# Attention probabilities transposed on VectorE in 32x32 blocks and regrouped by DMA, instead of on TensorE

## The chip, the cores and the metric

The kernel runs on one core of one Trainium2 chip. A core has five engines with instruction queues of their own: TensorE (PE, matrix products, with its weight loads shown as PEld), VectorE (DVE), ScalarE (ACT), GpSimd (POOL) and SyncE (SP), which here issues all DMAs. They work on one on-chip memory of 128 partitions (SBUF) and on a smaller accumulator memory (PSUM), in eight banks, that TensorE writes. The metric is the device time of one execution in microseconds (us); less is better.

## The reference

Eight batches of block-causal attention, eight heads of 64 columns over 576 positions in blocks of 64, followed by a gated feed-forward that also mixes positions. All data are float32.

```python
def _attn_ref(q, k, v):
    B, H, S, D = q.shape                      # 8, 8, 576, 64
    scores = 1.0 / np.sqrt(D) * np.matmul(q, k.transpose(0, 1, 3, 2))
    mask = block_i >= block_j                 # blocks of 64 positions
    scores = np.where(mask, scores, -1000000000.0)
    attn = np.exp(scores - np.max(scores, axis=-1, keepdims=True))
    attn = attn / (np.sum(attn, axis=-1, keepdims=True) + 1e-09)
    return np.matmul(attn, v)

def _moe_ref(x, w_in, w_spatial, b_spatial, w_out):
    h = np.maximum(x @ w_in, 0.0)             # 512 -> 1024
    u, v = h[..., :512], h[..., 512:]
    v_n = (v - mean(v)) / np.sqrt(var(v) + 1e-06)
    v_s = np.einsum('ts,bsd->btd', w_spatial, v_n) + b_spatial[None, :, None]
    return (u * v_s) @ w_out
```

## The kernel before

The work is cut into 32 head pairs (eight batches of four). For a pair the 576 query rows stand in four tiles of 128 and one of 64, and `SLOTS` lists seven pieces of score rows: for each of the two heads the tiles 0 and 1 together (slots 0 and 1), tile 2 (slots 2, 3), tile 3 (slots 4, 5), and for both heads together the last 64 rows (slot 6). Tile t needs only the first t + 1 blocks of 128 keys.

For each slot, `scores` (L265, and `scores_last`, L277) multiplies queries by keys into a PSUM bank `s`. In batch 0 it does so in float32 from the raw input; from batch 1 on `prep_pair` splits queries and keys into a high and a low part (`hi`, `lo`), and three products in float32r replace one. `exps` has DVE take the row minimum of the negated scores while it copies them to an SBUF tile `p` (L296, L305) and ACT apply the exponential with a running sum (L312). `norm` adds a small constant and inverts the sum on DVE (L321, L324) and has POOL scale `p` (L326). `p` then holds query rows in the partitions, but the product with `v` sums over keys, which must stand in the partitions. So `transposes` has TensorE turn each 128x128 block of `p` by a product with the identity (L352, L366) into a PSUM bank `t`; DVE (slots 0 and 1) or ACT copies the bank to the SBUF tiles `ptlo` and `pthi` (L354, L356, L361, and L367 for the last 64 keys). `av` multiplies them by `v` into the banks `avl` (query rows 0 to 255) and `avh` (256 to 575) (L396, L405), and `x_evac` brings these to the tile `x`, again as a high and a low part (L382, L383).

Once a batch's four pairs are there, `moe` makes a list of 29 groups of matrix products for its feed-forward: five `v_group` (bank `mv`; L436 and L447, then a relu, mean, variance and a scaling on L477, a cast to `vh` on L484 and the remainder `vl` on L485), eight `u_group` (bank `mu`, L505), eight `sp_group` (bank `ms`, L528, L532, L533; the mixing of positions) and eight `out_group` (bank `mo`, L549), whose results go out through `outT` (L555, L556).

The main loop walks over steps n, seven to a pair. A step issues one slot's `exps`, the `norm` of the slot before, the `transposes` of the slot before that, at certain steps scores or `av` (step 2 of the next pair, `RUN2`), loads, and about one feed-forward group of the batch before, so that the feed-forward of batch b runs between the attention of batch b + 1. In batch 0 there is no such work, and the weights are loaded and split in the background. The building framework, which orders each engine's instructions when the program is built, keeps roughly to this order but moves instructions where by its own account an operand comes late. On the chip each engine then works its list off in order. Tiles come from pools with a fixed number of buffers: seven for `p`, one for `ptlo` and `pthi`, one for the raw queries and keys, two for `v`, four PSUM banks for `s`, two for `t`, `avl` and `avh`, two for the feed-forward. A DMA is told finished by one of eight semaphores in turn, so that the ninth waits for the first.

Of the kernel before, what the change touches and what calls it, by code (L numbers as in the profile page):

```python
# [10 lines left out]
F32 = mybir.dt.float32  # L11
F32R = mybir.dt.float32r
I32 = mybir.dt.int32
AF = mybir.ActivationFunctionType
# [18 lines left out]
RUN2, LAST = 2, 5  # L33
# [3 lines left out]
def kernel(  # L37
# [25 lines left out]
    p_p = ctx.enter_context(tc.tile_pool(name="p_p", bufs=7))  # L63
    pt_p = ctx.enter_context(tc.tile_pool(name="pt_p", bufs=1))
# [36 lines left out]
    c4 = const.tile([P, P], F32, name="c4")  # L101
    nc.gpsimd.memset(c4[64:P, :], 0.0)
# [181 lines left out]
    def exps(b, pr, i):  # L284
# [3 lines left out]
        ssum = st_p.tile([P, 4], F32, tag="ssum", name=f"ssum_{nm}")  # L288
# [22 lines left out]
        for r, (o, n, mx) in enumerate(runs):  # L311
            nc.scalar.activation(  # L312
                pt[:, o:o + n], pt[:, o:o + n], AF.Exp, bias=mx, scale=-1.0,
                accum_out=ssum[:, r:r + 1],
            )
        ptiles[(b, pr, i)] = (pt, ssum, runs)

    def norm(b, pr, i):
        pt, ssum, runs = ptiles[(b, pr, i)]
        n = len(runs)  # L320
        nc.vector.tensor_scalar(  # L321
            out=ssum[:, 0:n], in0=ssum[:, 0:n], scalar1=EPS_SM, scalar2=None, op0=ALU.add
        )
        nc.vector.reciprocal(ssum[:, 2:2 + n], ssum[:, 0:n])  # L324
        for r, (o, n, mx) in enumerate(runs):
            nc.gpsimd.tensor_scalar(  # L326
                out=pt[:, o:o + n], in0=pt[:, o:o + n], scalar1=ssum[:, 2 + r:3 + r],
                scalar2=1.0, op0=ALU.mult, op1=ALU.mult,
            )

    pts = {}

    def pt_tiles(b, pr):
        if (b, pr) not in pts:
            lo = pt_p.tile([P, 2, 384], F32, tag="ptlo", name=f"ptlo_{b}_{pr}")
            hi = pt_p.tile([P, 2, 4, 320], F32, tag="pthi", name=f"pthi_{b}_{pr}")
            pts[(b, pr)] = (lo, hi)
        return pts[(b, pr)]

    def transposes(b, pr, i):  # L340
        hd, t0, t = SLOTS[i]
        pt = ptiles.pop((b, pr, i))[0]
        lo, hi = pt_tiles(b, pr)
# [5 lines left out]
        n = 3 if t == 1 else min(t + 1, 4)  # L349

        for c in range(n):
            nc.tensor.transpose(bk[:, c * P:(c + 1) * P], pt[:, c * P:(c + 1) * P], ident)  # L352
        if t == 1:
            (nc.scalar.copy if b == 0 else nc.vector.tensor_copy)(lo[:, hd, :], bk[:, 0:384])  # L354
        elif hd < 2:
            nc.scalar.copy(  # L356
                hi[:, hd, 0:n, (t - 2) * P:(t - 1) * P],
                bk[:, :n * P].rearrange("p (c q) -> p c q", q=P),
            )
        else:  # L360
            nc.scalar.copy(  # L361
                hi[:, :, :, 256:320].rearrange("p h c q -> p c h q"),
                bk.rearrange("p (c h q) -> p c h q", c=4, h=2),
            )
            bk = bank(f"{i}c4")
            nc.tensor.transpose(bk[0:64, 0:P], pt[:, 4 * P:S], ident)  # L366
            nc.scalar.copy(c4[0:64, :], bk[0:64, 0:P])  # L367
# [19 lines left out]
    def av(b, pr):  # L387

        lo, hi = pts.pop((b, pr))
# [3 lines left out]
        for c in range(2):  # L393
            for j in range(2):
                js = slice(64 * j, 64 * j + 64)
                nc.tensor.matmul(  # L396
                    al[js, c * P:256], vt[:, c, js],
                    lo[:, j, 0:256] if c == 0 else lo[:, j, 256:384],
                    start=(c == 0), stop=(c == 1),
                )  # L400
        for c in range(5):
            for j in range(2):
                js = slice(64 * j, 64 * j + 64)
                q0 = (0, 0, 0, 128, 256)[c]
                nc.tensor.matmul(  # L405
                    ah[js, q0:320], vt[:, c, js], hi[:, j, c, q0:] if c < 4 else c4[:, js],
                    start=(c == 0), stop=(c == 4),
                )
# [10 lines left out]
    def moe(b):  # L419
# [5 lines left out]
        def v_group(c):  # L425
# [16 lines left out]
            else:  # L442
# [34 lines left out]
            nc.vector.tensor_scalar(  # L477
                out=vr[:m, :], in0=vr[:m, :], scalar1=st[:m, 12:13], scalar2=st[:m, 13:14],
                op0=ALU.mult, op1=ALU.add,
            )  # L480
            if c < FULL:
                vh = ff_p.tile([P, DH], F32R, tag=f"vh{c}", name=f"vh_{b}_{c}")
                vl = ff_p.tile([P, DH], F32R, tag=f"vl{c}", name=f"vl_{b}_{c}")
                nc.vector.tensor_copy(vh, vr)  # L484
# [122 lines left out]
    def at(n):  # L607

        g, i = divmod(n, NS)
        return (*pairs[g], i) if 0 <= g < len(pairs) else None  # L610

    for n in range(N + 2 * NS):
# [17 lines left out]
        if at(n - 1):  # L630
            norm(*at(n - 1))
        if i == RUN2:
            if here:
                scores(*here, (4, 5))
            if 0 < g <= len(pairs):
                av(*pairs[g - 1])
                if g % NPAIR == 0:
                    gs = moe(pairs[g - 1][0])
                    queue += gs
                    rate = len(gs) / (NPAIR * NS)  # L640
# [8 lines left out]
        if at(n):  # L649
            exps(*at(n))  # L650
    for q in queue:
        q()
# [45 lines left out]
```

## Time and profile before

| | us |
|---|---|
| median of three runs | 773.93 |
| the three runs | 764.83, 773.93, 773.99 |
| the profiled execution | 765.58 |
| its span, first to last instruction | 763.8 |
| POOL busy in a steady batch (278.42 to 369.06) | 37.14 |
| granted TensorE clock, mean of the span | 0.996 |
| data moved by DMA | 48.63 MB, 64 GB/s |

A profile lists every instruction with its engine, its source line and its tiles as out<-in, its start and its duration, and for an engine that stood idle what ended the wait. Busy times of an engine are those in which it computes; a matmul's end is modelled, and following matmuls overlap, so that the sum of their durations is more than the time they take. The chain of waits follows the work that ended last back to its start, each step to what released it; there the times do add up. SPq is SP's list of DMA issues, which is not counted as busy.

### The profile page before, as it was taken

How to read it: one execution, taken by the hardware profiler on the slowest of the kernel's cores; microseconds unless marked ns; L12 is line 12 of the kernel's file. 1: busy time of each engine (PE TensorE's matmuls, PEld its weight loads, DVE VectorE, ACT ScalarE, POOL GpSimd, SP SyncE). 2: the span in 40 equal slices, each digit the busy share in tenths (PEclk: the TensorE clock that was granted, in tenths of full speed). 3: DMA queues.
4: the chain of work that ended last, by engine and by line, in shares of the span. 5: the costliest groups of instructions: out<-in, count | busy, mean ns of one | idle time of the engine just before them, and what ended most of it. 6: DMA issues, size and time to landing. Idle time of an engine off the chain costs nothing.

```text
span 763.8 us, 15854 instructions
## 1 busy us (share of the span) xinstructions
PE 740.3 (97%) x5508; PEld 636.0 (83%) x5508; DVE 471.9 (62%) x1743; ACT 436.1 (57%) x1236; POOL 318.4 (42%) x480
## 2 busy tenths in 40 slices
PE   8998889999999999999999999999999999999998
PEld 5556678987998878898888888898789987889898
DVE  6985984548745577547764577455874557742641
ACT  6885665656665556654655656564666555653232
POOL 4786465423444334442344423542344433431011
PEclk9999999999999999999999999999999999999999
DMA  6453231221122111221012211122112211000001
GB/s 215 151 170 103 84 98 33 75 82 34 52 69 72 42 51 51 69 71 58 18 51 82 78 38 50 30 71 84 33 52 73 67 42 51 18 33 32 1 9 55
DMA packets 21411, 48.63 MB, mean 64 GB/s; under 512 B 2386, under 2 KB 11090, under 8 KB 21332
## 3 DMA queue, kind: packets, MB, share of 16 engines
q1 hardware_dynamic: 21332, 47.63, 19.7%
q8 instruction: 44, 0.72, 0.4%
q14 instruction: 35, 0.29, 0.1%
HBM read 38.18 MB, written 9.44 MB: 62 GB/s over the span
## 4 chain that ended last, share of the span: by engine, by line
PE 81%; DVE 8%; ACT 5%; POOL 2%; issue 2%; DMA 1%; SPq 0%; ACTq 0%; DVEq 0%; POOLq 0%
PE mo L549 14%; PE ms L528 13%; PE mu L505 10%; PE t L352 10%; PE mv L436 10%; PE s L265 7%; PE avh L405 6%; PE s L277 3%; PE avl L396 2%; ACT p L312 2%; PE mv L447 1%; DVE st L457 1%; POOL p L326 1%; PE ms L533 1%; PE ms L532 1%
## 5 line engine op out<-in xcount | busy, mean ns | idle before, releaser
L326 POOL TENSOR_SCALAR p<-p,ssum 128x128 f32<-128x128 f32 (+4 forms) x288 | 177.9, 630 | 209.9 <-DVE ssum L324 173.9
L312 ACT ACTIVATE p<-p,nmax 128x128 f32<-128x128 f32 (+4 forms) x288 | 166.9, 581 | 59.6 <-DVE nmax L296 47.3
L296 DVE CUSTOM_DVE_ANT_0 p<-s,mask 128x128 f32<-128x128 f32 (+3 forms) x256 | 115.4, 484 | 62.8 <-PE s L265 62.7
L352 PE MATMUL t<-ident,p 128*128 128x128 f32 x768 | 124.6, 278 | 10.5 <-POOL p L326 7.2
L505 PE MATMUL mu<-x,wi_hi 128*128 128x288 f32 x512 | 116.5, 304 | 0.6 <-DVE vr L453 0.5
L352 PEld LDWEIGHTS t<-ident,p 128*128 128x128 f32 x768 | 90.6, 141 | 27.8 <-POOL p L326 12.3
L223 POOL TENSOR_TENSOR lo<-raw,hi 128x288 fp32r<-128x288 f32 (+1 forms) x84 | 66.9, 815 | 80.8 <-ACT hi L220 80.7
L436 PE MATMUL mv<-wi_hi,x 128*128 128x512 f32 x256 | 87.0, 401 | 0.0
L505 PEld LDWEIGHTS mu<-x,wi_hi 128*128 128x128 f32 x512 | 85.5, 188 | 1.4 <-DVE vr L453 0.7
L356 ACT COPY pthi<-t 128x512 f32<-128x512 f32 (+1 forms) x128 | 67.0, 525 | 29.1 <-PE t L352 28.8
L537 POOL TENSOR_TENSOR gl<-u,gh 128x288 fp32r<-128x288 f32 x48 | 38.7, 807 | 99.6 <-ACT gh L536 99.6
L528 PE MATMUL ms<-ws_hi,vh 128*128 128x288 f32 x256 | 80.0, 313 | 0.0
L535 DVE TENSOR_TENSOR u<-ms,u 128x288 f32<-128x288 f32 x64 | 29.3, 458 | 78.1 <-PE ms L533 78.0
L528 PE MATMUL ms<-ws_hi,vl 128*128 128x288 f32 x256 | 75.4, 294 | 0.0
L528 PE MATMUL ms<-ws_lo,vh 128*128 128x288 f32 x256 | 75.3, 294 | 0.0
L549 PE MATMUL mo<-gh,wo_hi 128*128 128x288 f32 x256 | 74.7, 315 | 0.0
L549 PE MATMUL mo<-gh,wo_lo 128*128 128x288 f32 x256 | 70.0, 295 | 0.0
L505 PE MATMUL mu<-x,wi_lo 128*128 128x288 f32 x256 | 69.7, 295 | 0.0
L536 ACT CAST gh<-u 128x288 fp32r<-128x288 f32 x64 | 27.8, 434 | 71.8 <-DVE u L535 71.8
L321 DVE TENSOR_SCALAR ssum<-ssum 128x1 f32<-128x1 f32 (+1 forms) x224 | 37.2, 166 | 50.8 <-ACT p L312 50.8
L405 PE MATMUL avh<-pthi,v 128*64 128x320 f32 (+1 forms) x512 | 67.9, 407 | 0.0
L405 PEld LDWEIGHTS avh<-pthi,v 128*64 128x64 f32 x512 | 36.0, 138 | 24.2 <-issue 0.3
(114 smaller groups left out, 1648.4 us busy)
## 6 DMA issues: line engine op xcount, KB each, us to landing
raw<-qk SPq DMA_DIRECT2D x31, 608.0 KB, 3.9
v<-v SPq DMA_DIRECT2D x32, 320.0 KB, 3.0
outT<-o SPq DMA_DIRECT2D x64, 144.0 KB, 1.8
rwi<-w_in SPq DMA_DIRECT2D x8, 512.0 KB, 4.6
rwo<-w_out SPq DMA_DIRECT2D x4, 512.0 KB, 3.7
rws<-w_spT SPq DMA_DIRECT2D x4, 288.0 KB, 2.7
rwt<-w_spT SPq DMA_DIRECT2D x2, 144.0 KB, 2.8
raw<-qk SPq DMA_DIRECT2D x2, 128.0 KB, 2.3
```

Source lines behind the costliest of these rows:

```text
L223: (nc.vector if n == 0 else nc.gpsimd).tensor_tensor(out=lo[:, cs], in0=raw[:, cs], in1=hi[:, cs].bitcast(F32), op=ALU.subtract)
L265: nc.tensor.matmul(banks[(b, pr, i + hd)][:, o:o + n], a[js, qs], k[js, :n], start=(m == 0), stop=(m == len(parts) - 1),)
L296: nc.vector.tensor_tensor_reduce(out=pt[:, o:o + n], in0=bk[:, o:o + n], in1=mask[:, 512 - n:], scale=-0.125, scalar=BIG, op0=ALU.add, op1 ...
L312: nc.scalar.activation(pt[:, o:o + n], pt[:, o:o + n], AF.Exp, bias=mx, scale=-1.0, accum_out=ssum[:, r:r + 1],)
L326: nc.gpsimd.tensor_scalar(out=pt[:, o:o + n], in0=pt[:, o:o + n], scalar1=ssum[:, 2 + r:3 + r], scalar2=1.0, op0=ALU.mult, op1=ALU.mult,)
L352: nc.tensor.transpose(bk[:, c * P:(c + 1) * P], pt[:, c * P:(c + 1) * P], ident)
L356: nc.scalar.copy(hi[:, hd, 0:n, (t - 2) * P:(t - 1) * P], bk[:, :n * P].rearrange("p (c q) -> p c q", q=P),)
L405: nc.tensor.matmul(ah[js, q0:320], vt[:, c, js], hi[:, j, c, q0:] if c < 4 else c4[:, js], start=(c == 0), stop=(c == 4),)
L436: nc.tensor.matmul(ps, xs[k][:, j, cs], w[:, k, DH:], start=(n == 0), stop=(n == 3 * NC - 1),)
L505: nc.tensor.matmul(ps[:, :HT], w[:, k, ds], xs[k][:, j, zs], start=(n == 0), stop=(n == 3 * NC - 1),)
L528: nc.tensor.matmul(ps[:, :HT], a[:, ds], w[:, k, zs], start=(n == 0), stop=False)
L549: nc.tensor.matmul(ps[:, :HT], w[:, k, es], a[:, k, :], start=(n == 0), stop=(n == 3 * ND - 1),)
```

## The change

From the second batch on TensorE transposes nothing. For those batches `transposes` has DVE transpose `p` in blocks of 32x32: each block is turned in place of its own 32 partitions, so what stands in partitions 32a to 32a + 31 comes from query rows 32a to 32a + 31, and the keys 32r to 32r + 31 of a block of 128 lie in column group r of the tiles `tlo` and `thi`. `exchange` then moves, for each of the four r and each of the four a, partitions 32a of column group r to partitions 32r, column group a of the tiles `dlo` and `dhi`: 16 DMAs each for the low part (slots 0 to 3) and the high part (slots 4 to 6), 32 a pair, from SBUF to SBUF, all issued by SP. In batch 0 `transposes_pe` still uses TensorE, and ACT writes its result in the new layout into the same `dlo` and `dhi`.

The other edits: `norm` and `transposes` take two slots at a time (the sums of the two heads share a tile), after the steps 1, 3, 5 and 6 of a pair. `av` reads `dlo` and `dhi` in runs of 32 columns, tile by tile, with 28 matmuls for 14, over the same number of columns, and is issued at step 4 of the next pair instead of 2 (`AV_AT`), in batch 0 still at 2. The ring of `p` has five buffers for seven; `tlo`, `thi`, `dlo` and `dhi` have one each. In `v_group` the scaling and the cast to `vh` go from DVE to ACT.

```diff
-RUN2, LAST = 2, 5
+RUN2, LAST, AV_AT = 2, 5, 4
+LB, HB = 6, 4
+LW, Q8O, HW = 2 * 32 * LB, 2 * 32 * HB, 2 * 32 * HB + 5 * 32
...
-    p_p = ctx.enter_context(tc.tile_pool(name="p_p", bufs=7))
-    pt_p = ctx.enter_context(tc.tile_pool(name="pt_p", bufs=1))
+    p_p = ctx.enter_context(tc.tile_pool(name="p_p", bufs=5))
+    tr_p = ctx.enter_context(tc.tile_pool(name="tr_p", bufs=1))
...
+    dlo = const.tile([P, 4, LW], F32, name="dlo")
+    dhi = const.tile([P, 4, HW], F32, name="dhi")
...
     def norm(b, pr, i):
+        both = [ptiles[(b, pr, j)] for j in ((i - 1, i) if i < NS - 1 else (i,))]
+        ssum = both[0][1]
+        n = sum(len(runs) for _, _, runs in both)
         nc.vector.tensor_scalar(
             out=ssum[:, 0:n], in0=ssum[:, 0:n], scalar1=EPS_SM, scalar2=None, op0=ALU.add
         )
-        nc.vector.reciprocal(ssum[:, 2:2 + n], ssum[:, 0:n])
+        nc.vector.reciprocal(ssum[:, 4:4 + n], ssum[:, 0:n])
...
+    def transposes(b, pr, i):
+        hd, t0, t1 = SLOTS[i]
+        pt = ptiles.pop((b, pr, i))[0]
+        if i == 0:
+            halves["lo"] = tr_p.tile([P, 4, LW], F32, tag="lo", name=f"tlo_{b}_{pr}")
+        if i == 4:
+            halves["hi"] = tr_p.tile([P, 4, HW], F32, tag="hi", name=f"thi_{b}_{pr}")
+        to, o, n = place(hd, t0)
+        to = halves["lo" if to is dlo else "hi"]
+        if t1 > t0:
+            n += t1 + 1
+        nc.vector.transpose(
+            to[:, :, o:o + 32 * n].rearrange("p r (c j) -> p c r j", j=32),
+            pt[:, :n * P].rearrange("p (c r j) -> p c r j", r=4, j=32),
+        )
+        if hd == 2:
+            nc.vector.transpose(
+                to[:, 0:2, Q8O + P:], pt[:, 4 * P:S].rearrange("p (r j) -> p r j", j=32)
+            )
+
+    def exchange(part):
+        t, d = halves[part], dlo if part == "lo" else dhi
+        for r in range(4):
+            w = LW if part == "lo" else HW if r < 2 else HW - 32
+            for a in range(4):
+                nc.sync.dma_start(d[32 * r:32 * r + 32, a, :w], t[32 * a:32 * a + 32, r, :w])
...
     def av(b, pr):
...
+        def tiles(t0, t1, c):
+            n = t1 - t0 + 1
+            out, q0 = (al, 0) if t1 < 2 else (ah, 2)
+            for j in range(2):
+                js = slice(64 * j, 64 * j + 64)
+                d, o, _ = place(j, t0)
+                o += 32 * c
+                nc.tensor.matmul(
+                    out[js, (t0 - q0) * P:(t1 + 1 - q0) * P].rearrange(
+                        "p (t a j) -> p a t j", a=4, j=32
+                    ),
+                    vt[:, c, js],
+                    d[:, :, o:o + 32 * n].rearrange("p a (t j) -> p a t j", j=32),
+                    start=(c == 0), stop=(c == t1),
+                )
...
-            nc.vector.tensor_scalar(
-                out=vr[:m, :], in0=vr[:m, :], scalar1=st[:m, 12:13], scalar2=st[:m, 13:14],
-                op0=ALU.mult, op1=ALU.add,
+            nc.scalar.activation(
+                vr[:m, :], vr[:m, :], AF.Identity, bias=st[:m, 13:14], scale=st[:m, 12:13]
             )
...
-                nc.vector.tensor_copy(vh, vr)
+                nc.scalar.copy(vh, vr)
...
-        if n >= 2 and at(n - 2):
-            transposes(*at(n - 2))
...
+        if at(n - 2) and at(n - 2)[0] > 0:
+            k = (i - 2) % NS
+            for j in (k - 1, k) if k in (1, 3, 5) else (k,) if k == 6 else ():
+                transposes(*at(n - 2)[:2], j)
+            if k in (3, 6):
+                exchange("lo" if k == 3 else "hi")
```

What this does to the order shows best on TensorE, VectorE and SyncE. Names carry the pair within the batch, then the slot or part (`t_2_0` is slot 0 of pair 2), and a running number.

TensorE before, in a steady batch: the whole `av` of pair 1 at one place, then the first transposes of pair 2 (`t`, from `p`) and a feed-forward group.

```order
L396 MATMUL avl_1_4036<-ptlo_1_3764,v_1_3299 64x256 x2
L396 MATMUL avl_1_4036<-ptlo_1_3764,v_1_3299 64x128 x2
L405 MATMUL avh_1_4037<-pthi_1_3765,v_1_3299 64x320 x6
L405 MATMUL avh_1_4037<-pthi_1_3765,v_1_3299 64x192 x2
L405 MATMUL avh_1_4037<-c_125,v_1_3299 64x64 x2
L352 MATMUL t_2_0_4060<-ident,p_2_0_3974 128x128 x3
L528 MATMUL ms_0_1_4065<-ws_hi,vh_0_3459 128x288
```

TensorE after, first place in the same batch: the part of pair 1's `av` that reads `dlo`, between two feed-forward groups.

```order
L588 MATMUL ms_0_2_4097<-ws_a,vs_a 128x288
L589 MATMUL ms_0_2_4097<-ws_b,vs_b 128x288
L444 MATMUL avl_1_4127<-dlo,v_1_3324 64x4x2x32 x2
L444 MATMUL avl_1_4127<-dlo,v_1_3324 64x128 x2
L444 MATMUL avh_1_4128<-dlo,v_1_3324 64x128 x6
L584 MATMUL ms_0_3_4163<-ws_hi,vh_0_3513 128x288
```

TensorE after, second place: the part that reads `dhi`, one `ms` group, the last scores of pair 2 and two `mo` groups later, among pair 3's first scores.

```order
L273 MATMUL s_3_2_4260<-hi_3_4009 128x384
L273 MATMUL s_3_3_4261<-hi_3_4009 128x384
L273 MATMUL s_3_2_4260<-lo_3_4010,hi_3_4009 128x384
L444 MATMUL avh_1_4128<-dhi,v_1_3324 64x128 x8
L461 MATMUL avh_1_4128<-dhi,v_1_3324 64x64 x10
L273 MATMUL s_3_3_4261<-lo_3_4010,hi_3_4009 128x384
```

The transposes are gone from TensorE's list, and `av` has become two pieces, each standing where its half of the exchange is expected. From the high part of one pair to that of the next there are, in this stretch, five `mo` groups, four `ms` groups, three runs of scores and one low part.

VectorE before, in the same batch: copies of slots 0 and 1 (`ptlo`) among the evacuations of `av` (`x`) and feed-forward work (`u`).

```order
L324 RECIPROCAL ssum_2_5_4186<-ssum_2_5_4186 128x1
L354 COPY ptlo_2_4058<-t_2_0_4060 128x384
L383 TENSOR_TENSOR x_1_4052<-avh_1_4037,x_1_4052 128x320
L535 TENSOR_TENSOR u_3426<-ms_0_1_4065,u_3426 128x288
L354 COPY ptlo_2_4058<-t_2_1_4093 128x384
```

VectorE after: the block transposes of pair 2's slots 4, 5 and 6 (`thi`), among the score reductions of pair 3 (`p`, `nmax`) and the evacuation of pair 1's `av`.

```order
L395 STREAM_TRANSPOSE thi_2_4310<-p_2_4_4183 128x4x4x32
L395 STREAM_TRANSPOSE thi_2_4310<-p_2_5_4211 128x4x4x32
L308 ISA p_3_1_4333,nmax_3_1_4332<-s_3_1_4259,mask 128x128
L308 ISA nmax_3_1_4332 128x1
L308 ISA p_3_1_4333,nmax_3_1_4332<-s_3_1_4259,mask 128x256
L308 ISA nmax_3_1_4332 128x1
L395 STREAM_TRANSPOSE thi_2_4310<-p_2_6_4254 128x4x4x32
L426 TENSOR_TENSOR x_1_4157<-avh_1_4128,x_1_4157 128x320
L400 STREAM_TRANSPOSE thi_2_4310<-p_2_6_4254 128x2x32
```

Copies from PSUM became transposes within SBUF, and the last of them stands behind the evacuation of an `av`.

SyncE before, in a steady batch: one load of queries and keys (`raw`) and one of `v` a pair, and the stores.

```order
L210 DMA raw_3_3947<-qk 128x1216
L232 DMA v_2_3641<-v 128x640
L210 DMA raw_0_4245<-qk 128x1216
L232 DMA v_3_3945<-v 128x640
L556 DMA outT<-o_0_0_4182 128x288
L210 DMA raw_1_4545<-qk 128x1216
```

SyncE after, in a steady batch, from one store to the next low exchange.

```order
L612 DMA outT<-o_0_0_2947 128x288
L410 DMA dlo<-tlo_2_2859 32x384 x6
L240 DMA v_3_2718<-v 128x640
L410 DMA dlo<-tlo_2_2859 32x384 x10
L612 DMA outT<-o_0_1_2989 128x288
L218 DMA raw_0_3022<-qk 128x1216
L612 DMA outT<-o_0_2_3040 128x288
L612 DMA outT<-o_0_3_3069 128x288
L410 DMA dhi<-thi_2_3050 32x416 x8
L410 DMA dhi<-thi_2_3050 32x384 x8
L410 DMA dlo<-tlo_3_3161 32x384 x6
```

Loads and stores now stand within and between the two exchanges of a pair, on the one list that SP works off in order; the load of `v` stands inside the low exchange and waits for a `v` buffer, which the high part of an `av` gives free.

More of the change, by code (lines that the diff above doesn't have):

```diff
@@ L287, in exps @@
         nmax = st_p.tile([P, 2], F32, tag="nmax", name=f"nmax_{nm}")
[L288 removed]
+        if hd == 1:
+            ssum = ptiles[(b, pr, i - 1)][1]
+        else:
+            ssum = st_p.tile([P, 8], F32, tag="ssum", name=f"ssum_{nm}")
+        s0 = hd * (t1 - t0 + 1) if hd < 2 else 0
         pt = p_p.tile([P, S], F32, tag="p", name=f"p_{nm}")
@@ L396, in av @@
                 nc.tensor.matmul(
[L397 to L406, printed above, removed]
+                    ah[js, 256:320].rearrange("p (a j) -> p a j", j=32), vt[:, c, js],
+                    dhi[:, 2 * j:2 * j + 2, Q8O + 32 * c:Q8O + 32 * c + 32],
                     start=(c == 0), stop=(c == 4),
```

95 lines of the change are left out of this document (49 added, 46 removed).

## The prediction

> **What bounds it now.** I read the page's busy times and its chain first, then the busy times by stretch, then the chain of waits in order of time inside one pair.
>
> ```profile
> span 763.8 us, 15854 instructions
> PE 740.3 (97%) x5508; PEld 636.0 (83%) x5508; DVE 471.9 (62%) x1743; ACT 436.1 (57%) x1236; POOL 318.4 (42%) x480
> PE 81%; DVE 8%; ACT 5%; POOL 2%; issue 2%; DMA 1%; SPq 0%; ACTq 0%; DVEq 0%; POOLq 0%
> ```
>
> TensorE (PE) is busy for 97% of the span and makes 81% of the chain that ended last. An average can hide stages, so the next view cuts the span where the first `av` of a batch starts. The columns are stretch, length, then busy time and count for PE, weight loads, DVE, ACT and POOL, then granted clock, DMA share and GB/s.
>
> ```profile
> 0.00:94.67 94.67, 82.39 (x463) 54.56 (x464) 74.47 (x278) 66.50 (x184) 61.06 (x83) 0.96 0.45 145
> 94.67:187.78 93.11, 89.77 (x697) 78.79 (x696) 59.63 (x218) 55.71 (x156) 45.50 (x68) 1.00 0.21 66
> 278.42:369.06 90.64, 89.82 (x695) 78.67 (x693) 56.24 (x214) 52.80 (x152) 37.14 (x59) 1.00 0.18 56
> 703.39:763.80 60.41, 56.76 (x389) 52.83 (x388) 23.43 (x59) 16.23 (x43) 5.13 (x7) 1.00 0.07 24
> ```
>
> The first stretch is mixed (PE idles 12 us). A steady batch lasts 90.64 us with PE idle for 0.8, DVE at 56.2 and DMA at 18%: there, an instruction taken from PE is time gained, as long as nothing else takes PE's place. The last stretch is feed-forward alone and has no transposes.
>
> The chain inside one pair of such a batch (start, length, engine and line) shows what a transpose costs next to its neighbours, which a busy time of overlapping matmuls can't.
>
> ```profile
> 302.22 0.48 PE t L352 x3
> 302.70 1.58 PE ms L528 x12
> 304.28 0.13 PE ms L532
> 304.41 0.14 PE ms L533
> 304.55 0.33 PE t L352 x3
> ...
> 308.89 0.79 PE s L277 x6
> 309.68 0.33 PE t L352 x3
> 310.01 1.58 PE mo L549 x12
> 311.59 0.44 PE t L352 x4
> ...
> 313.60 1.41 PE s L265 x17
> 315.00 0.59 PE t L352 x4
> ...
> 317.20 0.44 PE t L352 x4
> 317.63 0.11 PE t_6c L366
> ...
> 319.33 0.90 PE s L265 x4
> 320.23 0.80 PE avl L396 x8
> 321.03 2.05 PE avh L405 x20
> 323.09 0.26 PE t L352
> ```
>
> Three transposes take 0.33 us, four 0.44, the odd one 0.11. The 0.48 and 0.59 are the same groups behind an `av` and behind scores; I take the extra 0.15 as the price of leaving those, which whatever follows will pay.
>
> **The change, part by part.** *Transposes leave PE* in batches 1 to 7, 28 pairs. A pair has four groups of three (of the 0.33 rows there are three, the first and last shown, and the 0.48), three of four, and the odd one: 4 x 0.33 + 3 x 0.44 + 0.11 = 2.75 us, or 3.05 with the extras. 28 x 2.75 = 77 us off (85 at most). That the move happens isn't in doubt: from batch 1 on PE's order holds no transpose.
>
> *The value product `av`* streams the same 1600 columns per half-head pair, in 28 matmuls instead of 14. Rows: 1216 columns in 2.05 us, 1.69 ns each; the first 384 in 0.80, 2.08 ns each. At the first price nothing is added, at the second 0.6 us a pair. It now comes as two groups, so one more change of kind, 0.15. I take +0.25, 32 x 0.25 = +8, ends 0 and +20. No row shows a moving operand read in runs of 32 columns; at half speed it would cost 2.85 us a pair and eat the whole gain, but I have no row that suggests it.
>
> *DVE and ACT.* Rows give count, busy us and mean ns, by shape.
>
> ```profile
> L354 DVE COPY ptlo<-t 128x384 f32<-128x384 f32 x56 | 30.8, 551 | 22.7 <-PE t L352 22.7
> L477 DVE TENSOR_SCALAR vr<-vr,st 128x512 f32<-128x512 f32 x32 | 19.7, 617 | 0.6
> L484 DVE CAST vh<-vr 128x512 fp32r<-128x512 f32 x32 | 14.2, 443 | 0.6
> L321 DVE TENSOR_SCALAR ssum<-ssum 128x1 f32<-128x1 f32 x160 | 23.8, 149 | 41.5 <-ACT p L312 41.4
> L324 DVE RECIPROCAL ssum<-ssum 128x1 f32<-128x1 f32 x160 | 25.5, 160 | 4.0
> L296 DVE CUSTOM_DVE_ANT_0 p<-s,mask 128x512 f32<-128x512 f32 x64 | 42.2, 682 | 34.5 <-PE s L265 34.5
> L296 DVE CUSTOM_DVE_ANT_0 p<-s,mask 128x384 f32<-128x384 f32 x64 | 35.0, 549 | 0.1
> L150 DVE SCALAR_TENSOR_TENSOR fwo<-rwo,fwo 128x512 int32<-128x512 int32 x4 | 3.7, 922 | 0.0
> L356 ACT COPY pthi<-t 128x512 f32<-128x512 f32 x64 | 36.8, 575 | 3.1 <-PE t L352 3.0
> L441 ACT ACTIVATE vr<-mv 128x512 f32<-128x512 f32 x32 | 19.1, 597 | 51.4 <-PE mv L436 51.3
> ```
>
> Per batch DVE loses 8 copies (4.4 us), five scalings (about 3), four casts (1.8) and 12 of 28 add-and-reciprocal pairs of 0.31 (3.7): 12.9. It gains, per pair, four block transposes of 384 columns, three of 512 and one of 64. No row shows such a transpose. The ends are the 443 ns cast and the 922 ns three-operand form; I take the score reduction, the nearest single pass over as much data: 4 x 0.55 + 3 x 0.68 + 0.2 = 4.45 us, 17.8 per batch (12 to 27). So DVE goes from 56.2 to 61, of a batch of 90.64 - 4 x (2.75 - 0.25) = 80.6: room left, at the upper end 70, little. ACT loses 20 copies of up to 0.58 and gains nine passes of about 0.6: no more than before, 52.8 of 80.6, hidden behind PE.
>
> *The exchange* adds 32 DMAs per pair, all issued by SP, each 32 partitions of 1.5 KB. No DMA between SBUF addresses is in the trace. SP's issue times back to back (start, length, count), and landing times from issue:
>
> ```profile
> 0.72 1.81 SPq L208 DMA_DIRECT2D raw<-qk  x4
> 72.69 1.18 SPq L178 DMA_DIRECT2D rwt<-w_spT  x2
> 73.92 0.75 SPq L180 DMA_DIRECT2D rwt<-b_sp  x2
> outT<-o SPq DMA_DIRECT2D x64, 144.0 KB, 1.8
> rwt<-w_spT SPq DMA_DIRECT2D x2, 144.0 KB, 2.8
> ```
>
> One issue costs 0.45 (128 partitions), 0.59 (64) or 0.375 (one). I take 0.45, the row with most samples, and a landing of 2.0. With the raw load, the v load and two stores, 36 issues x 0.45 = 16.2 us of SP in a pair of 20.15 (80.6 / 4). It fits; at 0.59 it is 21.2 and doesn't.
>
> Busy time isn't enough, since SP serves in order. In a steady batch the `v` load of the pair after next stands inside the low exchange and waits for the high part of `av` (two v buffers). Behind it: 10 low DMAs, the raw load, three stores, then 16 high ones: 31 issues, 14.0 us, and 2.0 for landing: 16.0. In the same time PE has, from one high `av` to the next, five `mo` groups of 1.6, four `ms` of 1.85, scores of 0.90, 0.79 and 1.41, and 1.4 of low `av`: some 20 us. So the high exchange lands about 4 us early. The low one: 11 issues and landing, 6.95, against two `mo`, two `ms` and two scores, 8.6: 1.6 us early. Both hidden; without that cover each further microsecond stops PE.
>
> **A rule against the change.** The Trainium skill's page "VectorE: DVE Perf Modes" (section "Rules for kernel authors") advises TensorE for a 128x128 transpose whenever PSUM is an acceptable destination. By it the copies stay where they are and the sum is zero or a loss. For that to come true here DVE would have to become the bound: without transposes it has 43.3 us a batch, so they would have to take over 47 of 90.64, 2.6 times my rows; I count that within the chance of the DVE case below. The rows speak against it: PE has 0.8 us idle in a batch, DVE 34.
>
> **The sum**, against the profiled execution's own time of 765.58 us: -77 for the transposes, +8 for `av`. Batch 0 keeps its transposes and is not bound by PE: 0, ends -4 and +4 (12 small DVE pairs fewer; a ring of five probability tiles instead of seven). Batch 1 idles 3.3 us on weights, which won't shrink: +2. At the end the last high exchange (16 x 0.45 + 2.0 = 9.2) has only what feed-forward work can start without it: +2. In the steady batches closer engines and an in-order DVE that now waits for POOL before a transpose: +0.2 a pair, +6, ends 0 and 28. Sum 706.6, so 707 us. The median of the runs shown, 773.93, stands 1.1% above the profiled time; on that level the forecast is about 715.
>
> **Rivals.** *The exchange becomes the bound and the change is about even.* The loop runs from a high `av` through 31 issues and the landing to the next one, 31s + L + 1.4. It passes 20.15 at s = 0.54 with L = 2.0. At the 64-partition row (0.59, 2.8) it is 22.5 us, the old pair being 22.66: about 763. For it: the smaller transfer had the dearer issue. Against: one partition cost least.
>
> *The same loop, slower than before.* Above s = 0.595 (L = 2.8) a pair is longer than 22.66 whatever PE saves, and from 0.615 the loss passes 2%. If halving the partitions once more costs as much again as from 0.45 to 0.59, s = 0.73; at 0.65 the loop takes 24.4, 28 x 1.7 = 49 us more: 815. Nothing in the trace excludes it. The Trainium skill's page "DMA: Bandwidth & Descriptors" (section "Rules for kernel authors") says transfers under 64 KB are mostly overhead, and each DMA here moves 48 or 52 KB; the trace's four loads, issued 0.45 apart, show that such overheads overlap.
>
> *DVE.* If a block transpose costs like the 922 ns row, DVE has 70 of 80.6 us and its order makes PE wait for score banks; a microsecond a pair, 28 us: 735.
>
> **Chances.** Forecast 0.62, DVE 0.14, even 0.11, slower 0.13. The time is the forecast's, 707. The lower bound is the sum with every addition at its end of nothing, 688; upwards the range runs through the DVE case to the even one, 765, which leaves out the slower case, part of the even one and little below: 0.2. About 2% is what a measurement of this kernel can tell from no change, so faster takes the first two cases, 0.76; same 0.11; slower 0.13. For the forecast alone: 690 to 722.
>
> **What would show it.** Right: no L352-like rows after batch 0, a steady batch of 79 to 82 us, PE idle under 2 us in it, block transposes of 0.5 to 0.75 us, SP issues near 0.45. Wrong: PE idle in front of the high `av`, put down to a DMA; SP with gaps of 0.55 or more between issues; DVE above 65 us a batch; `av` above 3.2 us a pair.

## The result: slower by about 6%

The changed kernel takes 820.28 us (median of 4 runs, 814.8 to 823.25) against 770.23 for the kernel before on the same chips (4 runs, 764.83 to 773.99): a ratio of 1.0647, 95% interval [1.0547, 1.0748]. The forecast was 707 us, with a range up to 765. What came is nearest to the rival that the prediction called "the same loop, slower than before" and had put at 815 us for an issue of 0.65 us; how far that match goes is said under "The chances" below.

The head of the page of the changed kernel (busy time, share and instructions by engine) and its DMA issues (count, KB each, median us from issue to landing):

```profile
span 817.2 us, 17067 instructions
PE 722.1 (88%) x5704; PEld 612.6 (75%) x5704; DVE 501.2 (61%) x1647; ACT 424.2 (52%) x1140; POOL 307.3 (38%) x480
...
dlo<-tlo SPq DMA_DIRECT2D x448, 48.0 KB, 1.9
...
dhi<-thi SPq DMA_DIRECT2D x224, 52.0 KB, 2.3
dhi<-thi SPq DMA_DIRECT2D x224, 48.0 KB, 2.0
```

TensorE did lose its transposes, but its share fell from 97% to 88%: it now waits. The same columns as before, by stretch from one first `av` of a batch to the next, say where:

```profile
0.00:99.19 99.19, 87.32 (x575) 61.83 (x575) 76.09 (x246) 70.68 (x188) 58.35 (x82) 0.88 0.45 142
99.19:203.85 104.66, 92.42 (x705) 79.17 (x704) 66.61 (x215) 51.21 (x139) 42.63 (x66) 0.90 0.44 122
...
300.79:398.12 97.33, 86.16 (x705) 73.95 (x705) 61.03 (x206) 50.36 (x138) 35.77 (x58) 0.96 0.43 119
...
686.91:817.20 130.29, 113.12 (x907) 103.36 (x906) 54.83 (x167) 50.04 (x129) 27.14 (x43) 0.97 0.25 70
```

The first stretch is 4.5 us longer than before. Its 575 products, for 463, are mostly the smaller pieces of `av`, with two feed-forward groups more and 25 transposes fewer, so its edge lies a little later in the work. PE idles 11.9 us in it as against 12.3. A steady batch lasts 96.6 us on average (five from 203.85 to 686.91) against 90.64, with PE idle for 10 to 11 us instead of 0.8. DVE, at 61.0, has room.

What PE waits for, and what DVE waits for (engine, line, releaser: us in total, times, longest):

```profile
PE avl L444 <- DMA dlo<-tlo: 43.3, 8, 8.1
...
DVE tlo L395 <- DMA dlo<-tlo: 54.4, 19, 6.3
```

Both are the landing of the low exchange. That could be a slow transfer or a late issue; SP's list of issues between two low `av` of a steady batch (start, length from first to last, count) and PE's row behind it tell which:

```profile
441.20 10.30 SPq L410 DMA_DIRECT2D dhi<-thi  x16
451.61 3.70 SPq L410 DMA_DIRECT2D dlo<-tlo  x6
455.41 0.53 SPq L240 DMA_DIRECT2D v<-v  x1
455.98 6.20 SPq L410 DMA_DIRECT2D dlo<-tlo  x10
462.28 0.53 SPq L612 DMA_DIRECT2D outT<-o  x1
```

```profile
463.97 1.12 PE L444 MATMUL avl<-dlo,v 128*64 128x256 f32 x4 [5.10 <-DMA dlo<-tlo]
```

From 441.20 to 462.18 SP issues 33 DMAs without a pause, 20.98 us, 0.636 each. The last low one starts near 461.6 and lands 2 us later, and then `av` starts, 5.10 us after PE ran out of other work. The transfers are as quick as forecast (2.0 us); it is the issuing that is late.

That holds for all steady batches. From 203.85 to 686.91 the waits of SP's list add up to some 31 of 483 us; the longest of them, and the one for the high `av` in front of the `v` load, are:

```profile
SPq L612 <- ACT o L611: 11.7, 12, 1.8
...
SPq L240 <- PE avh L461: 0.7, 1, 0.7
```

So the queue itself is full: a pair of 24.15 us is 36 issues of 0.63 us, 22.7 us, and 1.5 us of waits.

### The profile page after: what moved, and what is told of

It is laid out like the page before. It is cut to its first block, busy times and chain, and to the rows that moved or that the text cites. A ratio compares the mean times of both kernels' runs of the same rounds, so it can differ in the third digit from the quotient of the medians.

```text
span 817.2 us, 17067 instructions
## 1 busy us (share of the span) xinstructions
PE 722.1 (88%) x5704; PEld 612.6 (75%) x5704; DVE 501.2 (61%) x1647; ACT 424.2 (52%) x1140; POOL 307.3 (38%) x480
## 5 line engine op out<-in xcount | busy, mean ns | idle before, releaser
L342 POOL TENSOR_SCALAR p<-p,ssum 128x128 f32<-128x128 f32 (+4 forms) x288 | 167.9, 598 | 119.0 <-DVE ssum L338 78.5
L561 PE MATMUL mu<-x,wi_hi 128*128 128x288 f32 x512 | 114.0, 303 | 11.1 <-ACT vr L498 6.6
L395 DVE STREAM_TRANSPOSE tlo<-p 128x384 f32<-128x384 f32 x112 | 60.9, 561 | 65.1 <-DMA dlo<-tlo 54.4
L444 PE MATMUL avl<-dlo,v 128*64 128x256 f32 (+1 forms) x256 | 32.6, 382 | 43.4 <-DMA dlo<-tlo 43.3
L470 POOL TENSOR_SCALAR xs<-x 128x128 fp32r<-128x128 f32 x32 | 10.3, 322 | 160.2 <-DVE x L426 160.2
L611 ACT COPY o<-mo 128x288 f32<-128x288 f32 x64 | 25.4, 397 | 83.7 <-DMA outT<-o 54.8
L493 PEld LDWEIGHTS mv<-wi_hi,x 128*128 128x128 f32 x256 | 49.2, 192 | 20.2 <-ACT x L425 5.4
L605 PEld LDWEIGHTS mo<-gh,wo_hi 128*128 128x128 f32 x256 | 48.9, 191 | 19.1 <-ACT gh L592 11.0
L395 DVE STREAM_TRANSPOSE thi<-p 128x512 f32<-128x512 f32 x84 | 54.1, 687 | 14.5 <-POOL p L342 4.8
L444 PEld LDWEIGHTS avl<-dlo,v 128*64 128x64 f32 x256 | 18.4, 154 | 56.4 <-issue 50.9
```

Of the source, the lines that this page charges most:

```text
L342: nc.gpsimd.tensor_scalar(out=pt[:, o:o + w], in0=pt[:, o:o + w], scalar1=ssum[:, r:r + 1], scalar2=1.0, op0=ALU.mult, op1=ALU.mult,)
L395: nc.vector.transpose(to[:, :, o:o + 32 * n].rearrange("p r (c j) -> p c r j", j=32), pt[:, :n * P].rearrange("p (c r j) -> p c r j", r=4, ...
L444: nc.tensor.matmul(out[js, (t0 - q0) * P:(t1 + 1 - q0) * P].rearrange("p (t a j) -> p a t j", a=4, j=32), vt[:, c, js], d[:, :, o:o + 32 * ...
L493: nc.tensor.matmul(ps, xs[k][:, j, cs], w[:, k, DH:], start=(n == 0), stop=(n == 3 * NC - 1),)
L561: nc.tensor.matmul(ps[:, :HT], w[:, k, ds], xs[k][:, j, zs], start=(n == 0), stop=(n == 3 * NC - 1),)
L605: nc.tensor.matmul(ps[:, :HT], w[:, k, es], a[:, k, :], start=(n == 0), stop=(n == 3 * ND - 1),)
```

## The experiments

Three theories stood against each other at first. A: SP's time to issue one DMA, about 0.63 us, is the bound, whatever the DMA carries. B: the data are the bound, that is the bytes, the landing or the short pieces. C: the other edits (block transposes on DVE, work moved to ACT, `av` in pieces) make the loss.

**Four wide copies for each exchange.** Column group r goes as it stands, all 128 partitions in one DMA: 8 DMAs a pair for 32, for nearly the same bytes (the last 32 columns of the high half are left out); the partitions aren't regrouped.

```diff
-            for a in range(4):
-                nc.sync.dma_start(d[32 * r:32 * r + 32, a, :w], t[32 * a:32 * a + 32, r, :w])
+            nc.sync.dma_start(d[:, r, :w], t[:, r, :w])
```

> Each exchange moves the same bytes with 4 DMAs over all 128 partitions instead of 16 over 32 (not regrouped, so the layout is not the one av wants; the last 32 columns of the high part are left out for all partitions). Theory A (SP's time to issue a DMA is the bound: 36 issues a pair, 0.63 us each for those of 32 partitions): 12 issues a pair at about 0.47, SP no longer matters, TensorE is the bound again, a steady batch of 79 to 82 us, 700 to 720 in all. Theory B (the data and their landing are the bound): the bytes stay, so the gain is half at most, above 760. Theory C (the other edits, DVE's order and TensorE's slower clock cost the time, not the exchange): no change, 800 to 825.

Measured: 739.97 us, beside 766.64 for the kernel before. One steady batch, and four of SP's issues in one row:

```profile
192.76:278.33 85.57, 81.37 (x705) 71.93 (x704) 61.33 (x205) 48.62 (x138) 35.06 (x58) 1.00 0.40 133
```

```profile
377.34 2.42 SPq L409 DMA_DIRECT2D dhi<-thi  x4
```

The batch falls from 96.6 to 85.57 us, and all the edits that C names are still in it, so C can't hold the bulk of the loss. The four issues still take some 0.6 us each (2.42 / 4), although each now has 128 partitions. But 740 isn't the 700 to 720 that A expected: A names the bound, and 20 us more are still to be explained (below).

One more thing differs, which the edit doesn't name. The building framework now places the high part of `av` straight behind the low one, which starts at 278.33 here; in the changed kernel it stands 14 us behind, after the low one at 439.68 (first row here, second there):

```profile
279.69 1.04 PE L443 MATMUL avh<-dhi,v 128*64 128x128 f32 x16
453.52 1.09 PE L444 MATMUL avh<-dhi,v 128*64 128x128 f32 x16
```

The gain could thus be partly one of order. The next run speaks against it: it has 32 DMAs again, the framework puts the two parts next to each other in about half of its pairs, and it is slow. In the runs after that the place varies too.

**The same count, wide.** 32 DMAs a pair again, each with 128 partitions and a quarter of the columns (no regrouping either).

```diff
-                nc.sync.dma_start(d[32 * r:32 * r + 32, a, :w], t[32 * a:32 * a + 32, r, :w])
+                nc.sync.dma_start(d[:, r, a * q:a * q + q], t[:, r, a * q:a * q + q])
```

> As many DMAs as in the change (32 a pair) and the same bytes, but each over 128 partitions and a quarter of the columns (not regrouped; the last 32 columns of the high part left out). Theory A with a price that hangs on the number of partitions: 0.47 per issue as for the 128-partition loads, 36 x 0.47 = 17 us a pair, 705 to 740. Theory A with a price for any DMA between SBUF addresses: 0.63 stays, 800 to 825. Theory B: quarter-size rows cost the DMA engines more, not less: 815 or above.

**A quarter of the bytes.** The DMAs of the change, with 96 columns each; the rest of `dlo` and `dhi` is not renewed.

```diff
-                nc.sync.dma_start(d[32 * r:32 * r + 32, a, :w], t[32 * a:32 * a + 32, r, :w])
+                nc.sync.dma_start(d[32 * r:32 * r + 32, a, :96], t[32 * a:32 * a + 32, r, :96])
```

> The 32 DMAs of 32 partitions a pair stay, but each moves 96 of 384 or 416 columns (three quarters of the regrouping is left out). Theory A: the number of issues and their 0.63 us stay, 805 to 825. Theory B: a quarter of the bytes, landings nearer 1.5 us than 2, SP waits less for its eight semaphores, below 760.

**Without the diagonal.** The 8 of the 32 DMAs that move partitions to themselves are left out.

```diff
+                if a != r:
-                nc.sync.dma_start(d[32 * r:32 * r + 32, a, :w], t[32 * a:32 * a + 32, r, :w])
+                    nc.sync.dma_start(d[32 * r:32 * r + 32, a, :w], t[32 * a:32 * a + 32, r, :w])
```

> The four DMAs of each exchange that keep their partitions (a equal to r) are left out: 24 a pair instead of 32. Theory A: 28 issues a pair x 0.63 = 17.7 us, plus waits of the order of those now, a pair of 20 to 21 instead of 24.3, 715 to 745. Theory B: a quarter of the bytes and landings goes too, but not the time of each: 780 to 800. Theory C: 805 to 825.

Measured: 842.05, 832.6 and 757.45 us, one run each. None is in A's bracket: the first is 17 us above it, at a time that B allows as well, the second 8 and the third 12 us above. What tells the theories apart is that a quarter of the bytes brings nothing where B expected less than 760, and the rows of issues. A row of 16 issues from each of the first two, and 12 from the third:

```profile
419.44 10.60 SPq L411 DMA_DIRECT2D dhi<-thi  x16
```

```profile
416.55 10.85 SPq L410 DMA_DIRECT2D dhi<-thi  x16
```

```profile
385.88 8.60 SPq L411 DMA_DIRECT2D dhi<-thi  x12
```

Sixteen issues take 10.3 us in the changed kernel, 10.60 with four times the partitions and a quarter of the columns, 10.85 with a quarter of the bytes (a few gaps included). A quarter of the bytes doesn't help at all, and a quarter fewer DMAs takes 63 us off the changed kernel's 820.28. B falls. The time goes by the number of DMAs, with the price of one the same from 12 to 192 KB and from 32 to 128 partitions. Why the first two are 12 to 22 us slower than the changed kernel isn't shown.

**Other queues.** In three runs other engines issued some of the 32. First ACT those with a = 3, 8 a pair:

```diff
-                nc.sync.dma_start(d[32 * r:32 * r + 32, a, :w], t[32 * a:32 * a + 32, r, :w])
+                (nc.scalar if a == 3 else nc.sync).dma_start(
+                    d[32 * r:32 * r + 32, a, :w], t[32 * a:32 * a + 32, r, :w]
+                )
```

> 8 of a pair's 32 regrouping DMAs are issued by ACT's queue. Theory A with a price of the issuing engine: SP 28 x 0.63 = 17.7 us of a pair, ACT gains 8 x 0.5 to 0.6 = 4 to 5 us a pair of instruction slots, in which its other work waits; 745 to 790 us, well below 820. Rival (the DMA engines or a shared ring are the limit, not the issuing queue): SP's interval grows as ACT's issues come in, 805 to 835 us.

785.78 us in one run: with the same DMAs and the same bytes 34 us below the changed kernel, so it is the issuing queue and not the engines that carry the data. The Trainium skill's page "DMA: Bandwidth & Descriptors" (section "Rules for kernel authors") says that spreading DMAs over issuing engines only saves sequencer issue time; here that saving was what counted, and it was worth those 34 us.

Then three queues, a = 2 by POOL and a = 3 by ACT:

```diff
+                (nc.sync, nc.sync, nc.gpsimd, nc.scalar)[a].dma_start(
```

> The 32 regrouping DMAs of a pair are issued by three queues: SP 16 (with its 4 loads and stores 20, at 0.63 us some 12 us of a pair), ACT 8 (at the 0.52 us seen with two queues, 4 us) and POOL 8. Theory A: no queue is the bound any more and the time comes to what the four wide copies gave, 740 to 760 us, below the 766 to 770 of the kernel before, if a POOL issue costs under 1 us. Rival Q (POOL's issues are dear, or its queue holds the normalisation of the probabilities up behind waits): 770 to 830 us, with TensorE waiting for POOL or for dhi.

770.99 us (10 runs) against 767.37: ratio 1.0036 [0.9993, 1.0079], no difference. That is 11 us above A's bracket, and at the lower edge of rival Q. Q's first reason fails, since POOL's issues were cheap (0.5 us each, by the first row below). Its second is not excluded: POOL stood 26.2 us in front of its own exchange issues (second row). PE's longest waits are not for POOL, though, but for ACT:

```profile
384.67 2.02 POOL L410 DMA_DIRECT2D dlo<-tlo  x4
```

```profile
POOL dhi L410 <- DVE thi L400: 26.2, 25, 1.3
```

```profile
PE mo L607 <- ACT gh L594: 12.9, 13, 2.1
PE ms L586 <- ACT o L613: 6.6, 8, 2.2
```

So the last of these left ACT alone: POOL issues a = 3 and half of a = 2, SP the other 20.

```diff
+                (nc.gpsimd if a == 3 or (a == 2 and r > 1) else nc.sync).dma_start(
```

> ACT issues none of the regrouping DMAs: SP 20 of a pair's 32 (24 with its loads and stores, 24 x 0.633 = 15.2 us of a pair, below the 20.15 us that the forecast wanted), POOL 12 (12 x 0.49 = 5.9 us beside its 9 us of work). Theory A2 (with three queues it was ACT's 8 issues, 8 x 0.54 = 4.3 us a pair, that made TensorE wait for ACT's gh and o): those waits fall from 12.9 and 6.6 us to under 4 each, a batch is 86 to 88 us and the run 740 to 760 us, faster than before by 1 to 4%. Rival: the waits move to the landing of dhi or to POOL's normalisation, 765 to 785 us, no gain.

777.92 us (6 runs) against 766.75: ratio 1.0136 [1.0092, 1.018]. The time is the rival's, no gain, though the waits it named (the landing of `dhi`, POOL) aren't the largest ones. PE's wait for `gh` falls to 7.1 us and the one for `o` goes from the head of the list, but others take their place:

```profile
PE mu L563 <- DVE vr L512: 8.3, 8, 3.2
PE mu L563 <- ACT u L568: 8.3, 7, 1.3
PE avh L446 <- DMA outT<-o: 7.1, 4, 2.1
PE mo L607 <- ACT gh L594: 7.1, 6, 2.1
```

A stretch of this run, 286.54 to 379.96, still lasts 93.42 us. That ACT's 8 issues were what kept three queues from a gain is therefore not borne out.

**Through DRAM.** Each exchange writes a scratch tile in DRAM with one DMA (the high half with a second, small one) and reads it back regrouped with four: 11 issues a pair for 32. Once with the rest as in the changed kernel, once with the scaling of `vr` and the cast `vh` back on DVE.

```diff
+        nc.sync.dma_start(h[:, :, :n if part == "lo" else n - 32], t[:, :, :n if part == "lo" else n - 32])
...
-            for a in range(4):
-                nc.sync.dma_start(d[32 * r:32 * r + 32, a, :w], t[32 * a:32 * a + 32, r, :w])
+            nc.sync.dma_start(d[32 * r:32 * r + 32, :, :w], h[:, r, :w].rearrange("(a x) w -> x a w", a=4))
```

> Each exchange goes through a scratch tile in DRAM: one 128-partition write (and a small second one for the last 32 columns of the high half), then four 32-partition reads in place of 16 copies, so 11 exchange issues per pair instead of 32. Theory A (SP's issue time was the bound, about 0.63 us a DMA): 11 x 0.63 = 7 us of a pair and 2 us for the loads, SP is free, and the time falls to what the four wide copies gave, 735 to 755 us. Rival L (the regrouping's latency is what counts): two landings in a row instead of one, some 4 us more for each exchange, so TensorE waits for the low and the high half each pair, about 2 to 4 us x 28, 790 to 850 us.

> As the run through DRAM, and the scaling and the cast of the stage behind (vr, vh) go back from ACT to VectorE. Theory ACT (what keeps the four wide copies at 740 and not 707 is ACT's extra passes, seen as TensorE's and SP's waits for ACT): 10 to 25 us below the run through DRAM, 715 to 735 us, and the waits of mu and ms for ACT's u shrink from 9.6 and 9.5 us to under 4 each. Rival (VectorE, at 68% busy, or the grouping in pairs sets the rest): within 5 us of the run through DRAM, or above it.

875.47 and 863.28 us against 769.85: ratios 1.1369 [1.1306, 1.1431] and 1.1193 [1.112, 1.1266]. Few issues, and yet the slowest kernels of all. Rival L held, and by more than it had said. Of the first: the landings, what SP waits for, and SP's issues around one low exchange:

```profile
hlo<-tlo SPq DMA_DIRECT2D x28, 768.0 KB, 5.0
dlo<-hlo SPq DMA_DIRECT2D x112, 192.0 KB, 4.6
hhi<-thi SPq DMA_DIRECT2D x28, 768.0 KB, 7.5
```

```profile
SPq L241 <- PE avh L471: 227.4, 30, 15.5
```

```profile
431.72 0.78 SPq L417 DMA_DIRECT2D dlo<-hlo  x2
442.48 0.35 SPq L241 DMA_DIRECT2D v<-v  x1
442.87 0.91 SPq L417 DMA_DIRECT2D dlo<-hlo  x2
```

Two landings in a row, of 4.6 to 7.5 us in these rows, replace one of 2.0, and the queue is served in order: after two reads of the low half SP stands for 10 us at the `v` load, which waits for the high `av` (two buffers for `v`), with the other two reads behind it. This `v` load stands inside the low exchange in the changed kernel as well; there PE reaches the high `av` early enough, and SP waited for it 20.5 us in the whole run, almost nothing in the steady batches. Bringing vr and vh back gave 12 us here, a difference that Theory ACT had named (10 to 25 us), though not the level (715 to 735); PE's longest wait, for ACT's `x`, falls from 36.6 to 25.6 us.

**What the other edits cost.** The rest of 33 us between the four wide copies (740) and the forecast (707) was to come from the edits that aren't the exchange. TensorE's transposes in all batches, all other edits kept; since `av` now stands behind the next pair's slots 0 and 1, it reads their low half in place of its own.

```diff
-        if at(n - 2) and at(n - 2)[0] == 0:
+        if at(n - 2):
...
-        if at(n - 2) and at(n - 2)[0] > 0:
+        if False:
```

> TensorE's transposes in all batches, every other edit kept (five probability buffers, division for two slots at once, the product with v in smaller pieces and two slots later, vr and vh on ACT): this prices the other edits without the exchange. By the forecast's sums: batch 0 nothing, product + 0.25 us x 32 pairs = 8, tail 2: 775 to 785 us against 766 to 770. If the other edits account for more of the loss (ACT copies the transposes as well): 790 to 810 us, and then the exchange alone costs the changed kernel only 10 to 30 us. If they cost nothing: 765 to 770 us.

The four wide copies with vr and vh on DVE, and the kernel before with only these two on ACT (the same lines in the other direction):

```diff
-            nc.scalar.activation(
-                vr[:m, :], vr[:m, :], AF.Identity, bias=st[:m, 13:14], scale=st[:m, 12:13]
-            )
+            nc.vector.tensor_scalar(
+                out=vr[:m, :], in0=vr[:m, :], scalar1=st[:m, 12:13], scalar2=st[:m, 13:14],
+                op0=ALU.mult, op1=ALU.add,
+            )
...
-                nc.scalar.copy(vh, vr)
+                nc.vector.tensor_copy(vh, vr)
```

> The four wide copies per exchange (the regrouping is left out, as there), with vr and vh back on VectorE. Theory ACT: ACT's extra passes make TensorE wait for u (4.2 us idle of a batch's 85.6); with them gone the batch is 82 to 84 us and the run 715 to 730 us. Rival V: VectorE, at 68%, then holds the same chain up instead, and the run stays at 735 to 755 us.

> The kernel before, with only vr and vh moved from VectorE to ACT. Forecast's value: nothing, 766 to 772 us. Theory ACT: ACT's delay shows where no exchange disturbs, 2 to 4 us a batch, 782 to 800 us.

Measured: 792.94 us against 769.85, ratio 1.0299 [1.0239, 1.0358]; 745.28 us in one run; 771.38 against 767.37, ratio 1.0053 [1.002, 1.0085]. The last two speak against ACT's extra passes as the cause of those 33 us: back on DVE they save nothing (one run, and PE's two longest waits for `u` stay at 9.5 and 9.0 us), and alone they cost 4 us, not the 12 to 34 that the theory named. The first shows a size: the other edits with TensorE's transposes cost 23 us, in the bracket of its second case, where the forecast's terms for them (+8 and +2) make 10. The changed kernel, with the block transposes and the exchange, takes 27 us more again. The first run's steady batch:

```profile
298.04:391.68 93.64, 91.69 (x805) 82.44 (x804) 47.35 (x173) 61.92 (x170) 35.82 (x58) 1.00 0.17 54
```

PE is busy for 91.69 us, 1.9 more than the 89.82 before, and idle for 1.95 instead of 0.8. ACT has 61.92 here, 9 more than before, since it makes all the copies out of the banks; part of the 23 us may be that and not the edits.

## Why the prediction was wrong, point by point

**The step that failed: "One issue costs 0.45 (128 partitions), 0.59 (64) or 0.375 (one). I take 0.45, the row with most samples".** The rows were loads from DRAM of the kernel before, and none showed a DMA between SBUF addresses, as the prediction said. The runs show 0.63 for such a DMA, with 32 or 128 partitions and 12 to 192 KB. So it isn't the partitions that set the price, on which the choice between 0.45 and 0.59 turned. 36 issues at 0.63 are 22.7 us of a pair, against 16.2 in the forecast and 20.15 to be had: the exchange doesn't fit, whatever PE saves.

**"Both hidden; without that cover each further microsecond stops PE."** The cover was gone, but not by the loop that the prediction drew. Its loop starts where the `v` load waits for the high `av`; 31 issues, landing and `av` give 31 x 0.633 + 2.0 + 1.4 = 23.0 us a pair by the measured price, and the pair takes 24.15 (96.6 / 4). In the steady batches SP waited for the high `av` once, for 0.7 us: the loop never closed, since the queue with all its 36 issues is the longer one. Of the 53.4 us between the two profiled spans, 29.8 lie in the five steady batches, 11.6 in batch 1 (104.66 us against 93.11), 7.5 in the last stretch and 4.5 in the first. The wait isn't where the prediction looked, in front of the high `av`, but in front of the low one, once a batch: the 16 issues of the high exchange stand ahead of the low one's, and the framework has placed the high `av` late. With wide or quarter-size copies, in the same number, PE's largest wait was at the high one (50.3 and 56.7 us); there the framework had placed it closer behind the low one.

**A second price was not in the sum.** A stall of PE was counted at its own length. Each of 5 to 6.5 us was followed by a stretch at half the clock (last section). PE's busy time of a steady batch is 85.5 to 86.3 us, against 81.4 with four wide copies. By the trace's clock PE is busy at half speed for 2.6 to 4.3 us of a batch, which by estimate accounts for 1.3 to 2.1 of those 4 to 5 us; where the rest comes from isn't shown.

**Transposes off PE, 77 us.** Right in kind, and near in size. With all other edits in place PE is busy for 91.69 us a batch with the transposes and, at a full clock, for 81.37 without them (four wide copies): 10.3 a batch of four pairs, where the forecast had 11. Against the kernel before, 89.82, the fall is only 8.45, where the forecast had 11 less 1 for `av`, that is 10.

**`av`, +0.25 us a pair.** Right as to its own size: where nothing holds it up it takes 2.98 us (319.24 to 322.22 in the run with TensorE's transposes in all batches; start, length, count). By the same reckoning it took 2.92 before (320.16 to 323.08); the prediction's 2.85 is the chain's length, which ends where the next product starts.

```profile
319.24 0.87 PE L444 MATMUL avl<-dlo,v 128*64 128x256 f32 x8
319.94 0.82 PE L444 MATMUL avh<-dlo,v 128*64 128x128 f32 x12
320.59 1.04 PE L444 MATMUL avh<-dhi,v 128*64 128x128 f32 x16
321.47 0.75 PE L461 MATMUL avh<-dhi,v 128*64 128x64 f32 x20
```

The moving operand in runs of 32 columns, in twice as many products, thus costs 0.06 us, almost nothing.

**DVE's block transposes, 0.55 and 0.68 us.** Right: the score reductions were the nearest row.

```profile
L395 DVE STREAM_TRANSPOSE tlo<-p 128x384 f32<-128x384 f32 x112 | 60.9, 561 | 65.1 <-DMA dlo<-tlo 54.4
...
L395 DVE STREAM_TRANSPOSE thi<-p 128x512 f32<-128x512 f32 x84 | 54.1, 687 | 14.5 <-POOL p L342 4.8
```

DVE has 60 to 61 us a batch, as the sum said, and the rival in which DVE becomes the bound falls. Its one weakness is seen in the first row: `tlo` has one buffer, so a late exchange also holds up DVE's next transposes.

**The waits of the steady batches, +6.** Too small. Where the issues don't bind (four wide copies) a batch is 85.57 us and not 80.6 + 0.8: PE is idle for 4.2 us instead of 1.6, and busy for 1.6 more than forecast. Over the five steady batches that makes 21 of the 33 us between 707 and 740. PE's waits there are many and short, the largest two for ACT's `u` (9.6 and 9.5 us in all); the run with vr and vh back on DVE left them as they were, and what causes them stays open.

**Batch 0, nothing, and the landing of 2.0 us.** Right as far as the runs can tell. The first feed-forward product starts at 68.21 us, before at 67.19, and at 71.33 in the run that moved only vr and vh and so has the old batch 0. A DMA of the exchange lands after 1.9 to 2.3 us by the page.

**The chances.** The resource that bound, SP's issuing, stood in the list with its condition (above 0.615 us), but had 0.13 because the sum took one row of another kind of DMA for the price. That this rival's 815 us lies so near to 820 is partly luck. It took 0.65 us and a landing of 2.8; with the measured 0.633 and 2.0 its own formula gives 23.0 us a pair, 0.4 above the old one, or some 776 us. The other 44 us lie in what it left out, among it the queue's five other issues of a pair and the half clock; no run divides them. A quantity on which a step from 0.45 to 0.65 turns a gain of 60 us into a loss of 50, and which no row shows, doesn't carry 0.62 for one value.

## What to carry to other kernels

Count the DMAs that one queue has to issue in a period, at the price of the same kind of DMA, before counting their bytes: at 0.63 us, 36 of them fill 22.7 us however little they move. Fewer DMAs help only if they don't lengthen the way: two landings through DRAM cost more than 21 saved issues, because the queue is served in order and a wait inside it stops what stands behind. Spreading the issues over three queues brought the time back to that of the kernel before, not below it, so none of the versions here is to be preferred to that kernel.

## What the runs showed of the hardware

*The issue of a DMA has a price that doesn't go by its size.* Between SBUF addresses SP took 0.63 us for one, in all of these runs, and POOL about 0.5. From DRAM the same queue took less: the four regrouped reads of one high exchange, 32 partitions with four runs each, show it.

```profile
453.19 1.74 SPq L417 DMA_DIRECT2D dhi<-hhi  x4
```

That is 0.44 each (1.74 / 4), where the four wide copies' row gave 0.61. The kind of DMA isn't all of it: the same `v` load is listed with 0.53 us between the DMAs of the changed kernel's low exchange and with 0.35 between the reads from DRAM. What makes the difference within the queue isn't shown.

*A stall of TensorE costs more than its length.* Around the 5.10 us stall at 463.97, in the same columns as the stretches above (the granted clock is the third number from the end):

```profile
455.00:458.80 3.80, 3.80 (x32) 2.99 (x27) 2.91 (x11) 1.84 (x5) 0.74 (x2) 1.00 0.55 151
458.80:464.00 5.20, 0.10 (x3) 0.06 (x3) 0.07 (x1) 0.81 (x2) 0.70 (x2) 0.71 0.41 100
464.00:467.40 3.40, 3.40 (x22) 2.65 (x23) 3.33 (x11) 1.53 (x4) 0.00 (x0) 0.50 0.84 283
467.40:474.20 6.80, 6.64 (x30) 4.88 (x28) 3.88 (x12) 3.79 (x10) 4.49 (x6) 0.97 0.33 92
```

The clock is 1.00 ahead of the stall and falls within it: 0.71 over those 5.20 us means some 2.2 us at the full clock and 3.0 at half. It is 0.50 for the 3.4 us behind it, and comes back. The Trainium skill's page "TensorE: Matmul & The Clock Gate" (section "What's actually happening") says that the gate halves the clock after an idle window of some 3.4 us and opens it after as long a busy one; the trace agrees in the direction and roughly in the size, but the clock here falls some 2.2 us into the stall, earlier than a whole idle window would have it. A wait that recurs once a batch thus costs, by estimate, its own 5 us and about half of the 3.4 us behind it.
